# Two rows of w4 loaded amid the V stream in transfers of few partitions, and one closing copy in place of two

## The chip, the cores and the metric

The kernel runs on one core of a Trainium2 chip. The metric is the device time of one execution in microseconds (us); lower is better. All times below are us unless marked ns. Engines are called by the profile's names: PE is TensorE, DVE is VectorE, ACT is ScalarE, SP is SyncE, which here issues nearly all transfers. "Transfer engines" are the core's 16 DMA engines.

## The reference: one decode step of attention beside an MLP

The computation is one decode step for four sequences: layer norm, sliding-window attention with 32 query heads over 16 key/value heads (the last 2048 positions of the cache), and an MLP, summed. Cut to what matters here:

```python
# B=4, D=576, Hq=32, Hkv=16, Dh=128, window W=2048, F=4608, all bf16
xn = layernorm(x)                                # both branches read xn
q = xn @ wq
p = softmax(q k^T / sqrt(128))                   # k, v: [4, 16, last 2048 of 8192, 128]
attn = (p v) @ wo                                # wo: [4096, 576]
x1 = xn              # S=1: all four shifted groups of the mixer are zero, w1 and w2 drop out
h2 = gelu(layernorm(x1) @ w3) @ w4               # w3: [576, 4608], w4: [4608, 576]
out = x + attn + (x1 + h2)
```

The kernel reads about 87 MB and writes 4.6 KB: K and V windows make 67 MB of it, the weights the rest.

## The kernel before

**Stages.** The program loads wq and computes the queries; streams the 16 K tiles (2 MB each, one per key/value head, `kv_load`, line 98), with the MLP's first weight w3 among them, and accumulates all scores; takes one softmax over everything; streams the 16 V tiles the same way; and finishes with the rest of w4, the MLP's second weight. In the text, V4 or V13 is the V tile of that head, and wo2 to wo7 are the 0.6 MB pieces of the attention's output weight, one for two heads.

**Order of issue.** All large loads are issued by SP in program order; SP waits in front of each until its buffer is free. K and V share six buffers (`NKV`, line 17). Each transfer also signals a completion semaphore; in the program as built, SP's transfers use eight of these in turn, and an issue waits until the previous transfer on its semaphore has landed. This is the framework's doing and stands nowhere in the kernel's text. Counting back from V15 (line 438), the order is V10, wo5, V11, V12, wo6, V13, V14, wo7, V15.

**The V loop** (lines 435 to 443) issues tile v+4 while it computes head v: `v_compute` (64 matmuls), then `head_out`, whose later parts (selecting, projecting with wo into the accumulator `ACC`) are run one head later by `run_later`.

**w4.** It is held as two halves e of 18 rows per partition (`w4_src`, line 106). One "row" here is [128 partitions x 576] bf16, 1152 B per partition, 147 KB in all. `load_w4(e, i0, n, cuts)` (line 396) allocates one of the three buffers of pool `w` and issues one transfer per cut; `mlp_out` (line 407) multiplies each row into `ACC` by two matmuls (line 330). Nine rows are used before the softmax; at the end (line 444) come three loads: 9 rows, 9 rows, and 9 rows cut into 4, 2, 2, 1, named w4_0_9, w4_1_0 and w4_1_9 in the text by half and first row.

**The end.** After the last piece two copies move `ACC` (f32, 36 x 288) to `fin` (bf16): the left half by DVE, the right half by ACT (lines 456 and 457). Then SP and ACT each store one half of the output (line 459).

Of the kernel before, what the change touches and what calls it, by code (L numbers as in the profile page):

```python
# [11 lines left out]
BF16 = mybir.dt.bfloat16  # L12
# [9 lines left out]
def kernel(  # L22
# [18 lines left out]
    nc = tc.nc  # L41
    P = 128
    B, Sq, D = A_x.shape
# [19 lines left out]
    DH = D // 2  # L63
# [24 lines left out]
    wpl = ctx.enter_context(tc.tile_pool(name="w", bufs=NWP))  # L88
# [9 lines left out]
    def kv_load(win, h):  # L98
        t = kvp.tile([P, NCH, Dh], BF16, tag="kv")
        nc.sync.dma_start(out=t[:].rearrange("p c d -> p (c d)"),  # L100
                          in_=win[:, h].rearrange("b (p c) d -> p b (c d)", p=G))
        return t
# [3 lines left out]
    w4_src = B_w4.rearrange("(e m i) n -> e m i n", e=2, i=NFH)  # L106
# [72 lines left out]
    ACC = ps_acc.tile([P, 512], F32)  # L179
# [46 lines left out]
    for y in range(NY):  # L226
        tq = ps_o.tile([P, 2 * HB, P], BF16, tag="O", name=f"tq{y}")
        for k in range(2):
            for m in range(HB):
                nc.tensor.transpose(out=tq[:, k * HB + m, :],  # L230
                                    in_=q_rows[:, k, m, y, :, :].rearrange("p g i -> p (g i)"), identity=ident[:])
# [41 lines left out]
    def softmax():  # L273
        E = wpl.tile([P, NCH, NG, GK], F32, tag="w", name="E")
        mx = const.tile([P, NG], F32)
        nb = const.tile([P, 1], F32)
        sm = const.tile([P, NG], F32)
        for g in range(NG):
            nc.vector.reduce_max(out=mx[:, g:g + 1], in_=S[g][:], axis=AX.X)  # L279
        nc.vector.reduce_max(out=nb[:], in_=mx[:], axis=AX.X)  # L280
        nc.vector.tensor_scalar_mul(out=nb[:], in0=nb[:], scalar1=-scale)  # L281
        for g in range(NG):
            nc.scalar.activation(out=E[:, :, g, :].rearrange("p (c l) k -> p c k l", l=2),  # L283
                                 in_=S[g][:].rearrange("p (c k l) -> p c k l", k=GK, l=2), func=ACT.Exp, bias=nb[:], scale=scale, accum_out=sm[:, g:g + 1])
        rd = const.tile([P, 1], F32)
        nc.vector.tensor_reduce(out=rd[:], in_=sm[:], op=ALU.add, axis=AX.X)
        nc.vector.reciprocal(out=rd[:], in_=rd[:])
        rdm = const.tile([P, B], F32)
        nc.vector.tensor_scalar_mul(out=rdm[:], in0=mask[:], scalar1=rd[:])  # L289

        PZ = pzp.tile([P, NCH, P], BF16, tag="pz", name="PZ")
        HC = CP // 2
        for piece in range(NP):
            c0 = piece * CP
            pr = ktp.tile([P, CP, NG, GK, B], BF16, tag="kt", name=f"pr{piece}")
            for b in range(B):
                src = E[:, c0:c0 + CP, :, :].rearrange("p c g k -> p (c g k)")
                dst = pr[:, :, :, :, b].rearrange("p c g k -> p (c g k)")
                if b == 3 or (b == 1 and piece % 2):
                    nc.scalar.mul(out=dst, in_=src, mul=rdm[:, b:b + 1])  # L300
                else:
                    nc.vector.tensor_scalar_mul(out=dst, in0=src, scalar1=rdm[:, b:b + 1])  # L302
            for half in range(2):
                tp = ps_s.tile([P, HC, P], BF16, tag="S", name=f"pt{piece}{half}")
                for cc in range(HC):
                    nc.tensor.transpose(out=tp[:, cc, :],  # L306
                                        in_=pr[:, half * HC + cc, :, :, :].rearrange("p g k b -> p (g k b)"),
                                        identity=ident[:])
                dst = PZ[:, c0 + half * HC:c0 + (half + 1) * HC, :].rearrange("p c n -> p (c n)")
                src = tp[:].rearrange("p c n -> p (c n)")  # L310
                if half:
                    nc.scalar.copy(out=dst, in_=src)  # L312
                else:
                    nc.vector.tensor_copy(out=dst.bitcast(I32), in_=src.bitcast(I32))
        return PZ

    O_tiles = {}

    def v_compute(h):
        bank = ps_o.tile([P, 128], F32, tag="O", name=f"O{h}")  # L320
        O = bank[:, 0:B * rep].rearrange("p (b r) -> p b r", r=rep)
        O_tiles[h] = (O, bank[:, 64:64 + XR * rep * B].rearrange("p (x n) -> p x n", x=XR))
        vn = V_tiles.pop(h)
        for c in range(NCH):
            nc.tensor.matmul(out=O, lhsT=vn[:, c, :], rhs=PZ[:, c, :].rearrange("p (b n) -> p b n", b=B)[:, :, h * rep:(h + 1) * rep],  # L325
                             start=(c == 0), stop=(c == NCH - 1))
# [9 lines left out]
    def load_wo(g2):  # L336
        wo_tiles[g2] = wop.tile([P, XR, D], BF16, tag="wo", name=f"wo{g2}")
        nc.sync.dma_start(out=wo_tiles[g2][:].rearrange("p x n -> p (x n)"), in_=wo_src[:, g2, :])
# [3 lines left out]
    def head_out(h):  # L342


        O, T = O_tiles.pop(h)
        on = small.tile([P, rep, B], BF16, tag="on")
        nc.vector.tensor_copy(out=on[:].rearrange("p r b -> p b r"), in_=O)  # L347

        def select():
            for x in range(XR):  # L350
                nc.tensor.matmul(out=T[0:32, x, :], lhsT=ident[:, x:P:XR], rhs=on[:].rearrange("p r b -> p (r b)"),  # L351
                                 start=(x == 0), stop=(x == XR - 1), skip_group_check=True)
            g2, odd = divmod(h, 2)
            if not odd:
                onx_tiles[g2] = small.tile([P, XR, B], BF16, tag="onx", name=f"onx{g2}")
            onx = onx_tiles[g2]
            for r in range(rep):
                q = 32 * (2 * odd + r)
                nc.vector.tensor_copy(out=onx[q:q + 32, :, :], in_=T[0:32, :, r * B:(r + 1) * B])  # L359
            if odd:  # L360
                wt = wo_tiles.pop(g2)
                onx_tiles.pop(g2)

                def project():
                    for x in range(XR):
                        acc_matmuls(onx[:, x, :], lambda a, z, x=x: wt[:, x, a:z])
                later.append(project)
        later.append(select)

    def run_later():  # L370
        fns = later[:]
        later.clear()
        for fn in fns:
            fn()
# [21 lines left out]
    def load_w4(e, i0, n, cuts):  # L396
        t = wpl.tile([P, n, D], BF16, tag="w", name=f"w4_{e}_{i0}")
        parts = []
        a = 0
        for m in cuts:  # L400
            nc.sync.dma_start(out=t[:, a:a + m, :], in_=w4_src[e, :, i0 + a:i0 + a + m, :])
            parts.append((t[:, a:a + m, :], e, i0 + a, m))
            a += m
        assert a == n
        return parts

    def mlp_out(t, e, i0, n):
        for i in range(n):
            acc_matmuls(gT[:, e * NFH + i0 + i, :], lambda a, z, i=i: t[:, i, a:z])
# [22 lines left out]
        load_wo(g2)  # L432
    mlp_out(*w4[0])
    PZ = softmax()
    for v in range(Hkv):
        n = v + NV0
        if n < Hkv:
            V_tiles[n] = kv_load(v_win, n)
            if n % 2 == 0:
                load_wo(n // 2)  # L440
        run_later()
        v_compute(v)
        head_out(v)
    end = load_w4(0, 9, 9, (9,)) + load_w4(1, 0, 9, (9,)) + load_w4(1, 9, 9, (4, 2, 2, 1))
    run_later()
    mlp_out(*end[0])
    while later:
# [4 lines left out]

    fin = const.tile([P, DH], out.dtype)
    NR = 32 + B
    HH = DH // 2
    nc.vector.tensor_copy(out=fin[0:NR, 0:HH], in_=ACC[0:NR, 0:HH])  # L456
    nc.scalar.copy(out=fin[0:NR, HH:DH], in_=ACC[0:NR, HH:DH])  # L457
    for q, eng in ((0, nc.sync), (1, nc.scalar)):
        eng.dma_start(out=o2[:, q * DH:(q + 1) * DH], in_=fin[32 * q:32 * q + B, :])

# [29 lines left out]
```

## Time and profile before

| what | value |
|---|---|
| median of 3 runs | 217.47 us (217.23 to 218.13) |
| the profiled execution's own time | 217.53 us |
| its span, first to last instruction | 215.8 us |
| transferred | 87.52 MB, mean 406 GB/s |
| PE busy, DVE busy, ACT busy | 53%, 50%, 10% of the span |
| V tile, issue to landing (median of 16) | 29.1 us |
| mean granted PE clock | 0.668 |

The span is what the profile sees; the execution's time has 1.7 us around it. In the profile's rows, "SPq" is an issue by SP, "<-" after a bracketed number names what ended the engine's idle time, and a "granted clock" of 0.5 means that PE ran at half its speed in that stretch. A transfer is split into packets, here one per partition, and each transfer engine that took part marks its end by a completion record. A 128-partition transfer leaves 16 such records, and it has landed when the last one is there.

In the stretch tables the columns are: the stretch, its length, busy time of PE, of PE's weight loads, of DVE, ACT and POOL (with the number of instructions), the granted clock, the DMA share and GB/s.

### The profile page before, as it was taken

How to read it: one execution, taken by the hardware profiler on the slowest of the kernel's cores; microseconds unless marked ns; L12 is line 12 of the kernel's file. 1: busy time of each engine (PE TensorE's matmuls, PEld its weight loads, DVE VectorE, ACT ScalarE, POOL GpSimd, SP SyncE). 2: the span in 40 equal slices, each digit the busy share in tenths (PEclk: the TensorE clock that was granted, in tenths of full speed). 3: DMA queues.
4: the chain of work that ended last, by engine and by line, in shares of the span. 5: the costliest groups of instructions: out<-in, count | busy, mean ns of one | idle time of the engine just before them, and what ended most of it. 6: DMA issues, size and time to landing. Idle time of an engine off the chain costs nothing.

```text
span 215.8 us, 5535 instructions
## 1 busy us (share of the span) xinstructions
PE 114.9 (53%) x2577; PEld 74.2 (34%) x2577; DVE 108.7 (50%) x156; ACT 21.3 (10%) x37; POOL 1.8 (1%) x8
## 2 busy tenths in 40 slices
PE   0343788847544544455433097867662635445383
PEld 0110744526311111111101087747452534334341
DVE  7932968484999999989785591201000000000000
ACT  0202220000000000000003896000000000000000
POOL 1110000000000000000000000000000000000000
PEclk9999999658566665678578566555555555555559
DMA  6999999999999999999999999999999999999960
GB/s 250 431 427 424 418 429 444 409 436 416 427 422 434 416 425 431 416 434 437 403 438 422 434 406 428 430 419 428 413 431 427 405 436 415 436 418 426 415 253 14
DMA packets 8255, 87.52 MB, mean 406 GB/s; under 512 B 925, under 2 KB 1065, under 8 KB 2729
## 3 DMA queue, kind: packets, MB, share of 16 engines
q1 hardware_dynamic: 8216, 87.17, 96.0%
q8 instruction: 20, 0.33, 0.6%
q10 hardware_dynamic: 16, 0.01, 0.0%
q14 instruction: 3, 0.02, 0.0%
HBM read 87.17 MB, written 0.00 MB: 404 GB/s over the span
## 4 chain that ended last, share of the span: by engine, by line
DMA 70%; DVE 13%; PE 7%; ACT 5%; issue 3%; SPq 1%; DVEq 0%; ACTq 0%
DMA t<-in_A_k_cache_dram 36%; DMA t<-in_A_v_cache_dram 21%; DMA w<-in_B_w_dram 9%; DVE kt L258 6%; DMA wq<-in_A_wq_dram 3%; PE O L325 2%; ACT E L283 2%; PE pt L306 2%; ACT pr L300 2%; DVE qz L177 2%; PE qp L204 1%; ACT PZ L312 1%; DVE mx L279 1%; DVE pr L302 1%; PE ACC L330 1%
## 5 line engine op out<-in xcount | busy, mean ns | idle before, releaser
L258 DVE STREAM_TRANSPOSE kt<-t 128x2048 int32<-128x2048 int32 x32 | 72.3, 2293 | 12.6 <-DMA t<-in_A_k_cache_dram 12.4
L267 PE MATMUL S<-kt,qz 32*32 32x512 bf16 x1024 | 36.9, 625 | 37.7 <-DVE kt L258 36.2
L325 PE MATMUL O<-PZ,t 128*128 128x8 bf16 x1024 | 30.5, 168 | 26.2 <-DMA t<-in_A_v_cache_dram 22.8
L325 PEld LDWEIGHTS <-t 128*128 128x128 bf16 x1024 | 29.1, 104 | 30.2 <-DMA t<-in_A_v_cache_dram 25.4
L347 DVE CAST on<-O 128x8 bf16<-128x8 f32 x16 | 2.7, 167 | 58.0 <-PE O L325 57.9
L267 PEld LDWEIGHTS <-qz 32*32 32x32 bf16 x1024 | 10.7, 95 | 60.3 <-issue 57.1
L306 PE MATMUL pt<-ident,pr 128*128 128x128 bf16 x64 | 6.7, 291 | 9.4 <-DVE pr L302 8.3
L383 PEld LDWEIGHTS <-w 128*128 128x128 bf16 x144 | 9.3, 165 | 5.2 <-DMA w<-in_B_w_dram 2.7
L383 PE MATMUL ACC<-ln2T,w 128*128 128x4 bf16 x144 | 9.6, 202 | 1.8 <-DMA w<-in_B_w_dram 1.8
L330 PE MATMUL ACC<-wo,onx 128*4 128x288 bf16 x64 | 9.0, 437 | 2.2 <-DVE onx L359 2.2
L283 ACT ACTIVATE E<-S,nb 128x512 f32<-128x512 f32 x4 | 4.0, 1116 | 59.3 <-DVE nb L281 59.3
L306 PEld LDWEIGHTS <-pr 128*128 128x128 bf16 x64 | 5.9, 135 | 10.0 <-ACT pr L300 10.0
L300 ACT ACTIVATE pr<-E,rdm 128x512 bf16<-128x512 f32 x6 | 8.1, 1430 | 0.8 <-DVE rdm L289 0.8
L359 DVE CAST onx<-O 32x16 bf16<-32x16 f32 x32 | 5.3, 165 | 5.3 <-PE O L351 4.9
L457 ACT CAST fin<-ACC 36x144 bf16<-36x144 f32 x1 | 0.3, 273 | 77.4 <-DVE fin L456 77.4
L330 PE MATMUL ACC<-w,gT 128*4 128x288 bf16 x72 | 7.3, 362 | 0.9 <-DMA w<-in_B_w_dram 0.9
L302 DVE TENSOR_SCALAR pr<-E,rdm 128x512 bf16<-128x512 f32 x10 | 6.4, 787 | 0.3 <-PE pt L306 0.2
L204 PE MATMUL qp<-wq,xnT 128*4 128x512 bf16 x32 | 4.0, 620 | 4.5 <-DMA wq<-in_A_wq_dram 4.5
L224 DVE CAST q_rows<-qp 128x256 bf16<-128x256 f32 x8 | 2.9, 410 | 6.4 <-PE qp L204 6.4
L351 PE MATMUL O<-on,ident 128*32 128x8 bf16 x64 | 4.2, 171 | 3.6 <-DVE on L347 3.6
L351 PEld LDWEIGHTS <-ident 128*32 128x32 bf16 x64 | 4.4, 111 | 3.4 <-issue 3.1
L330 PEld LDWEIGHTS <-gT 128*4 128x4 bf16 x72 | 3.9, 103 | 4.7 <-issue 2.2
(68 smaller groups left out, 54.5 us busy)
## 6 DMA issues: line engine op xcount, KB each, us to landing
t<-in_A_k_cache_dram SPq DMA_DIRECT2D x16, 2048.0 KB, 24.7
t<-in_A_v_cache_dram SPq DMA_DIRECT2D x16, 2048.0 KB, 29.1
w<-in_B_w_dram SPq DMA_DIRECT2D x4, 1152.0 KB, 13.1
wo<-in_A_wo_dram SPq DMA_DIRECT2D x8, 576.0 KB, 21.5
wq<-in_A_wq_dram SPq DMA_DIRECT2D x4, 1024.0 KB, 6.3
w<-in_B_w_dram SPq DMA_DIRECT2D x3, 1296.0 KB, 30.4
w_t<-in_B_w_dram SPq DMA_DIRECT2D x1, 576.0 KB, 14.3
w<-in_B_w_dram SPq DMA_DIRECT2D x1, 576.0 KB, 25.2
```

The source lines that it names most:

```text
L204: nc.tensor.matmul(out=qp[k][32 * i:32 * i + B, :], lhsT=lhsT, rhs=rhs, start=False, stop=False, skip_group_check=True)
L258: nc.vector.transpose(out=ap32(kt, e * G * 2, [[2 * G * 2, NCH // 2], [1, 2], [2, G]]), in_=ap32(kn, e * G, [[2 * 2 * G, NCH // 2], [2 * G ...
L267: nc.tensor.matmul(out=S[g][32 * b:32 * b + 32, :].rearrange("p (c k l) -> p c k l", k=GK, l=2), lhsT=qz[32 * g:32 * g + 32, b, h, y, :], ...
L283: nc.scalar.activation(out=E[:, :, g, :].rearrange("p (c l) k -> p c k l", l=2), in_=S[g][:].rearrange("p (c k l) -> p c k l", k=GK, l=2), ...
L300: nc.scalar.mul(out=dst, in_=src, mul=rdm[:, b:b + 1])
L302: nc.vector.tensor_scalar_mul(out=dst, in0=src, scalar1=rdm[:, b:b + 1])
L306: nc.tensor.transpose(out=tp[:, cc, :], in_=pr[:, half * HC + cc, :, :, :].rearrange("p g k b -> p (g k b)"), identity=ident[:])
L325: nc.tensor.matmul(out=O, lhsT=vn[:, c, :], rhs=PZ[:, c, :].rearrange("p (b n) -> p b n", b=B)[:, :, h * rep:(h + 1) * rep], start=(c == 0 ...
L330: nc.tensor.matmul(out=ACC[32 * q:32 * q + B, 0:DH], lhsT=lhsT, rhs=rhs_cols(q * DH, (q + 1) * DH), start=False, stop=False, skip_group_ch ...
L351: nc.tensor.matmul(out=T[0:32, x, :], lhsT=ident[:, x:P:XR], rhs=on[:].rearrange("p r b -> p (r b)"), start=(x == 0), stop=(x == XR - 1), ...
L359: nc.vector.tensor_copy(out=onx[q:q + 32, :, :], in_=T[0:32, :, r * B:(r + 1) * B])
L383: nc.tensor.matmul(out=gp[:, fc, :], lhsT=lhsT, rhs=rhs, start=False, stop=False, skip_group_check=True)
```

## The change

Rows 16 and 17 of w4's second half are no longer loaded at the end. A buffer `w4_end` is allocated before the V loop, and ahead of V10 and of V13 one row each is loaded into it, split by partitions into transfers of 8, 4, 12, 2, 6 and 96 partitions, and of 10, 14, 1, 3, 5, 7 and 88. At the end the remaining seven rows of the half are loaded in cuts of 4, 2 and 1; the two early rows are multiplied after w4_1_0 and before the 4-row piece. The two closing copies become one on DVE over all 288 columns. No value of the result is computed differently.

```diff
@@ the V loop
+    end_t = wpl.tile([P, 9, D], BF16, tag="w", name="w4_end")
+    groups = {10: (8, (8, 4, 12, 2, 6, 96)), 13: (7, (10, 14, 1, 3, 5, 7, 88))}
     for v in range(Hkv):
         n = v + NV0
+        if n in groups:
+            i, parts = groups[n]
+            p0 = 0
+            for k in parts:
+                nc.sync.dma_start(out=end_t[p0:p0 + k, i, :], in_=w4_src[1, p0:p0 + k, 9 + i, :])
+                p0 += k
+            assert p0 == P
         if n < Hkv:
             V_tiles[n] = kv_load(v_win, n)
...
-    end = load_w4(0, 9, 9, (9,)) + load_w4(1, 0, 9, (9,)) + load_w4(1, 9, 9, (4, 2, 2, 1))
+    end = load_w4(0, 9, 9, (9,)) + load_w4(1, 0, 9, (9,)) + [(end_t[:, 7:9, :], 1, 16, 2)]
+    for a, m in ((0, 4), (4, 2), (6, 1)):
+        nc.sync.dma_start(out=end_t[:, a:a + m, :], in_=w4_src[1, :, 9 + a:9 + a + m, :])
+        end.append((end_t[:, a:a + m, :], 1, 9 + a, m))
...
-    HH = DH // 2
-    nc.vector.tensor_copy(out=fin[0:NR, 0:HH], in_=ACC[0:NR, 0:HH])
-    nc.scalar.copy(out=fin[0:NR, HH:DH], in_=ACC[0:NR, HH:DH])
+    nc.vector.tensor_copy(out=fin[0:NR, :], in_=ACC[0:NR, 0:DH])
```

## The prediction

> **What bounds the kernel now.** First the page's chain and its row of transfer-engine shares.
>
> ```profile
> DMA  6999999999999999999999999999999999999960
> q1 hardware_dynamic: 8216, 87.17, 96.0%
> q8 instruction: 20, 0.33, 0.6%
> DMA 70%; DVE 13%; PE 7%; ACT 5%; issue 3%; SPq 1%; DVEq 0%; ACTq 0%
> ```
>
> The transfer engines are full from the second slice almost to the end, so time is bytes plus whatever leaves an engine without work. All 16 do not end together; the stretches of the tail show it:
>
> ```profile
> 204.00:206.00 2.00, 1.02 (x23) 0.81 (x22) 0.50 (x3) 0.00 (x0) 0.00 (x0) 0.50 1.02 416
> 206.00:208.00 2.00, 2.00 (x22) 1.07 (x18) 0.00 (x0) 0.00 (x0) 0.00 (x0) 0.50 0.68 272
> 208.00:210.00 2.00, 2.00 (x20) 1.10 (x18) 0.00 (x0) 0.00 (x0) 0.00 (x0) 0.50 0.49 184
> 210.00:212.00 2.00, 1.78 (x28) 1.01 (x24) 0.00 (x0) 0.00 (x0) 0.00 (x0) 0.99 0.15 51
> ```
>
> The last two columns are the DMA share and GB/s: from 208 on half of the engines have nothing left. The completion records of the last transfer agree: eight engines between 207.00 and 207.98, five at 210.1 to 210.4 or 211.6, three more by 211.93. The lateness comes in steps of about 1.57: a 16 KB instruction packet (q8) takes 1.02 to 1.11 on its engine, and the data packet after it 1.08 to 1.16 where 16 KB otherwise takes 0.61. The q8 durations repeat with period eight, so eight engines share the 20 fetches, two or three each. The latest engine sets the end.
>
> Third, SyncE's issues beside TensorE's work.
>
> ```profile
> 172.26 1.87 PE L325 MATMUL O<-PZ,t 128*128 128x8 bf16 x64 [0.97 <-DMA t<-in_A_v_cache_dram]
> ...
> 172.23 0.54 SPq L100 DMA_DIRECT2D t<-in_A_v_cache_dram  x1
> ...
> 186.18 0.33 SPq L401 DMA_DIRECT2D w<-in_B_w_dram  x1
> ```
>
> The first is head 10's compute, released by V10's landing at 172.21. The second is the issue of V15, with no matmul that it needs: it waits for the same landing. The program as built gives SP's transfers eight completion semaphores in turn, so each issue waits until the transfer eight places earlier has landed. V15 is eight after V10; the third row, a two-row piece of w4, is eight after wo6 and dates wo6's landing: 186.16. Eight in flight are now mostly 2 MB each, so nothing runs dry.
>
> **The change, part by part.** Thirteen small transfers take places in that ring of eight, although they hold 0.29 MB together.
>
> *First group (6, before V10).* V10's issue now follows wo4's landing (162.39) instead of 148.0. 0.54 to issue and some 0.6 to its first packet give 163.5; the earliest engine ends V9 at 163.84 by its completion, so nothing is lost there. One row spread evenly is 8 packets of 1152 B at 0.051 = 0.41 per engine, ahead of all that follows: wo6 lands near 186.6.
>
> *Second group (7, after wo6, before V13).* Places back from V13: seven small ones, then wo6. V13 may be issued only when wo6 has landed, and behind wo6 there is nothing in the queues but small rows. Before, V13 was issued at 161.00, 25 us ahead. Behind it on SP stand V14, wo7, V15 and all of w4's end, and TensorE, done with head 12 by 188, waits for V13. Now every engine runs out: the early ones from about 182, the latest at 186.6. The price from landing to effective restart is bounded by two rows. The program's first load (wq_t, 0.5 MB, idle engines) lands 3.4 after its issue by the page; its packets are 8 of 0.159 = 1.27 per engine: 2.1 of fixed time, and 2.2 with V's issue of 0.54 for 0.42. The closing store took 1.44 from issue (212.93) to landing with 0.04 of packets: 1.4, or 1.6 with V's issue. [...] I take 1.9, between the rows and nearer the load, which is the same sort of transfer. Bounds 0.9 to 2.2.
>
> *What is late next.* All 16 engines restart level. Work from V13 to the end is, per engine, 24 packets of 16 KB at 0.6135 (14.7), wo7 1.43, two times 8 x 0.389 (6.2), and 8 packets each of 0.1785, 0.0935 and 0.0515 (2.6): 25.0. Before, the engine that was latest at wo6 had had its third fetch, and no more. In the records three fetches come after 188 (188.97, 199.87, 209.18), on engines that were 1.4 us earlier. Level engines lose that lead, so one fetch, 1.57, comes on top. End of transfers: 186.6 + 1.9 + 25.0 + 1.57 = 215.1, against 211.93 now: +3.15. Without the fetch on top (it falls in the dry stretch) 213.5; with the restart at its bounds 214.1 to 215.4.
>
> [...]
>
> *Last pieces.* w4's end transfers are 4, 2, 1 rows instead of 4, 2, 2, 1. The two early rows are multiplied after w4_1_0 and before the 4-row piece.
>
> ```profile
> 208.73 2.64 PE L330 MATMUL ACC<-w,gT 128*4 128x288 bf16 x30
> 211.59 0.67 PE L330 MATMUL ACC<-w,gT 128*4 128x288 bf16 x6 [0.22 <-DMA w<-in_B_w_dram]
> 212.30 0.30 DVE L456 CAST fin<-ACC 36x144 bf16<-36x144 f32 x1 [7.00 <-PE ACC L330]
> 212.63 0.27 ACT L457 CAST fin<-ACC 36x144 bf16<-36x144 f32 x1 [77.41 <-DVE fin L456]
> ```
>
> TensorE is nearly the bound there: 36 matmuls after w4_1_0 with 0.22 idle. A row (two matmuls) takes 0.24 by the records' starts at granted clock 0.5 and 0.12 at 1.0, which came at 210.1. After the change the last piece lands 2.6 after w4_1_0 instead of 3.24 (two rows less to transfer), with the same 18 rows to multiply. These need 4.3 at 0.5 throughout and 2.2 at 1.0, so TensorE may end 0.33 (as now) to 1.7 after the last landing. With the clock rising midway, 0.75: +0.4. Bounds 0 to +1.4.
>
> *Closing copy.* Two 36x144 copies run one behind the other, 212.30 to 212.91 = 0.61. VectorE's casts of 8, 144 and 256 f32 columns take 0.167, 0.301 and 0.410, 0.98 ns a column; 288 come to 0.44. Gain 0.17, on the path.
>
> SP's extra issues (some 13 x 0.38 = 5 us) cost nothing by themselves: SP waits for landings meanwhile. The buffer of w4_end is free since the MLP's first stage.
>
> *Sum.* 3.15 + 0.4 - 0.17 = +3.4 on the profiled execution's 217.53 (span 215.8 and 1.7 around it): 220.9. The shown median, 217.47, is the same within 0.1.
>
> **Rivals.**
> 1. *The restart is paid, but no fetch falls on top.* For it: one fetch came at 188.97, close to the dry stretch. Against: two more follow on other engines. +3.4 - 1.57: 219.3.
> 2. *The wait is hidden*: wo6 lands early enough, or the rows cover it, and lateness among engines absorbs it. For it: eight engines have 3 to 5 us to spare. Against: the latest has none. Only the tail moves, +0.4 - 0.17 at most: 217.5.
> [...]
> 4. *The tail on a cold TensorE*: clock 0.5 to the end, +1.0 beyond mine: 221.9. In the profile the clock stayed at 0.5 for 78 us before 210.1.
>
> **How the numbers follow.** Forecast 220.9, 0.68; rival 1 0.10; rival 4 0.10; rival 2 0.08; rival 3 0.04. The range starts at rival 1 less 0.4 for the tail's bound, 218.9, and ends at rival 4 with the restart's upper bound, 222.2; it leaves out rivals 2 and 3. 0.5% of the time, 1.1 us, is what a measurement can tell from no change. Slower 0.88, same 0.10 (rival 2 and most of rival 3), faster 0.02.
>
> **What would show it.** V13's issue right after wo6's landing near 186.6, its landing near 193.5 to 195 instead of 191.2; a slice near 182 to 188 with the DMA share far below full; completions of wo7 almost level; the last landing near 215; fewer than 0.5 us from TensorE's end to the output's issue. Wrong if V13 is issued well before 180, or if the DMA share shows no gap.

## The result, and the profile after

| | before | after |
|---|---|---|
| median, same chip (4 runs each) | 217.62 us (217.23 to 218.13) | 221.39 us (221.21 to 221.50) |
| profiled execution, its span | 217.53, 215.8 | 221.50, 219.7 |
| last landing | 211.93 | 215.85 |
| PE's end, output's issue | 212.26, 212.93 | 216.62, 217.14 |
| mean granted PE clock | 0.668 | 0.664 |

The change makes the kernel slower by 3.77 us, a ratio of 1.0168 with a 95% interval of 1.0151 to 1.0184. The profiled execution lost 3.97.

The page after, as before: the share of the transfer engines and their GB/s in 40 slices of 5.5 us, and the chain that ended last.

```profile
DMA  6999999999999999999999999999999995799990
GB/s 260 447 404 437 418 429 433 411 421 433 422 424 430 424 430 424 427 424 420 437 425 427 430 411 429 424 418 426 424 383 374 428 424 211 299 430 424 416 373 6
...
DMA 66%; DVE 13%; PE 11%; ACT 4%; SPq 2%; issue 2%; DVEq 0%; ACTq 0%
```

Two slices that were full before stand at 5 and 7 tenths, and 211 and 299 GB/s: 181 to 192 us. A smaller dent is in the GB/s alone, 383 and 374 in the slices of 159 to 170, where the DMA share stays at 9: engines are busy there and move less. The chain's shares hardly tell of it: DMA 66% instead of 70, PE 11 instead of 7, and waiting at issues (SPq and issue) 4 as before. The place is found in the slices.

The stretches around the dent in the changed kernel (columns as before: the clock, the DMA share and GB/s are the last three):

```profile
180.00:184.00 4.00, 2.65 (x74) 2.37 (x76) 0.50 (x3) 0.00 (x0) 0.00 (x0) 0.50 0.86 355
184.00:188.00 4.00, 2.73 (x74) 2.10 (x70) 0.17 (x1) 0.00 (x0) 0.00 (x0) 0.50 0.27 91
188.00:190.00 2.00, 0.00 (x0) 0.00 (x0) 0.33 (x2) 0.00 (x0) 0.00 (x0) 0.50 0.78 270
190.00:196.00 6.00, 1.46 (x54) 1.46 (x55) 0.00 (x0) 0.00 (x0) 0.00 (x0) 0.50 1.02 431
...
212.00:214.00 2.00, 2.00 (x20) 1.02 (x18) 0.00 (x0) 0.00 (x0) 0.00 (x0) 0.50 0.92 345
214.00:216.00 2.00, 2.00 (x26) 1.28 (x24) 0.00 (x0) 0.00 (x0) 0.00 (x0) 0.68 0.05 19
```

The engines run out from 182 on, and from 184 to 188 they work a quarter of the time. The last two rows are the other half of the story: before, the tail from 206 on went 272, 184, 51 GB/s, as engines finished one after the other; now it is nearly full to 214, and almost nothing is left after.

Who made the dent stands in SyncE's timeline (start, duration, engine, line, operation, tiles, count; a long duration is an issue that waits):

```profile
170.28 0.58 SPq L338 DMA_DIRECT2D wo<-in_A_wo_dram  x1
170.92 14.93 SPq L444 DMA_DIRECT2D w_end<-in_B_w_dram  x7
186.96 1.61 SPq L100 DMA_DIRECT2D t<-in_A_v_cache_dram  x2
188.68 0.57 SPq L338 DMA_DIRECT2D wo<-in_A_wo_dram  x1
189.30 0.54 SPq L100 DMA_DIRECT2D t<-in_A_v_cache_dram  x1
```

wo6 is issued, then the seven small pieces, and V13 only at 186.96, 0.01 after the last completion of wo6 (186.95). V14, wo7 and V15 follow at once, since they had only stood behind it. Before, V13 and V14 had been issued 26 us earlier:

```profile
161.00 2.47 SPq L100 DMA_DIRECT2D t<-in_A_v_cache_dram  x2
```

And what the wait does to TensorE:

```profile
185.59 1.87 PE L325 MATMUL O<-PZ,t 128*128 128x8 bf16 x64 [0.99 <-DMA t<-in_A_v_cache_dram]
...
194.54 1.87 PE L325 MATMUL O<-PZ,t 128*128 128x8 bf16 x64 [6.57 <-DMA t<-in_A_v_cache_dram]
```

The first row is head 12, the second head 13: 6.57 idle, released by V13's landing (194.50). The completions of V13 lie within 0.48 of each other, where wo6's were 3.66 apart: the dry stretch has levelled the engines.

The tail:

```profile
213.31 2.21 PE L330 MATMUL ACC<-w,gT 128*4 128x288 bf16 x18
215.35 1.27 PE L330 MATMUL ACC<-w_end,gT 128*4 128x288 bf16 x18
216.66 0.45 DVE L468 CAST fin<-ACC 36x288 bf16<-36x288 f32 x1 [6.83 <-PE ACC L330]
217.14 0.30 SPq L470 DMA_DIRECT2D out_dram<-fin  x1
```

The second row holds the eighteen matmuls of the last nine rows, four of them for the two early rows, which landed long ago. TensorE comes to them only at 215.35, behind w4_1_0, and ends 0.78 after the last landing (215.85). One copy of 0.45 stands where two stood, and the output is issued 0.52 after TensorE's end instead of 0.67.

### The profile page after: what moved, and what is told of

Same layout as the page of the kernel before. It is cut to its first block, busy times and chain, and to the rows that moved or that the text cites. A ratio compares the mean times of both kernels' runs of the same rounds, so it can differ in the third digit from the quotient of the medians.

```text
span 219.7 us, 5546 instructions
## 1 busy us (share of the span) xinstructions
PE 114.5 (52%) x2577; PEld 73.3 (33%) x2577; DVE 108.9 (50%) x156; ACT 21.1 (10%) x36; POOL 1.8 (1%) x8
## 4 chain that ended last, share of the span: by engine, by line
DMA 66%; DVE 13%; PE 11%; ACT 4%; SPq 2%; issue 2%; DVEq 0%; ACTq 0%
DMA t<-in_A_k_cache_dram 35%; DMA t<-in_A_v_cache_dram 18%; DMA w<-in_B_w_dram 9%; DVE kt L258 6%; PE O L325 3%; PE ACC L330 3%; DMA wq<-in_A_wq_dram 3%; PE pt L306 2%; ACT E L283 2%; DVE qz L177 2%; PE qp L204 1%; ACT PZ L312 1%; ACT pr L300 1%; DVE mx L279 1%; DVE pr L302 1%
## 5 line engine op out<-in xcount | busy, mean ns | idle before, releaser
L306 PE MATMUL pt<-ident,pr 128*128 128x128 bf16 x64 | 5.5, 259 | 9.0 <-DVE pr L302 7.6
L306 PEld LDWEIGHTS <-pr 128*128 128x128 bf16 x64 | 4.9, 118 | 9.9 <-ACT pr L300 9.9
L330 PE MATMUL ACC<-w,gT 128*4 128x288 bf16 x54 | 6.8, 436 | 0.7 <-DMA w<-in_B_w_dram 0.7
L330 PEld LDWEIGHTS <-onx 128*4 128x4 bf16 x64 | 3.8, 110 | 4.3 <-DVE onx L359 2.6
```

The source lines that it names most:

```text
L306: nc.tensor.transpose(out=tp[:, cc, :], in_=pr[:, half * HC + cc, :, :, :].rearrange("p g k b -> p (g k b)"), identity=ident[:])
L330: nc.tensor.matmul(out=ACC[32 * q:32 * q + B, 0:DH], lhsT=lhsT, rhs=rhs_cols(q * DH, (q + 1) * DH), start=False, stop=False, skip_group_ch ...
```

## The experiments

Two theories stood at first. The **ring theory**: the thirteen small transfers cost by the places that they take among SP's eight completion semaphores, and only the second group does, by making V13 wait for wo6. Its rival: **the small transfers cost by themselves**, by their spread over few engines or by the partitions that they reach. A third question was the tail. "Small" is said of a piece of a row of w4; each difference is against the kernel before on the same chip (its medians there were 217.48 and 217.70).

**1. The two rows, each in one transfer.** Same bytes, places and tail, no split.

```diff
-    groups = {10: (8, (8, 4, 12, 2, 6, 96)), 13: (7, (10, 14, 1, 3, 5, 7, 88))}
+    groups = {10: (8, (128,)), 13: (7, (128,))}
```

> The two early rows come as one 128-partition transfer each, at the same places; everything else as in the changed kernel. Ring theory (thirteen small transfers fill the eight places in flight, so V13 waits for wo6 and all engines run dry): V13's issue goes back to about 161 to 164, no slice of the DMA share falls below 9 before 206, the last landing is near 211.9 and the time 217.3 to 217.8 (before, less 0.17 for the copy, plus 0 to 0.4 for the longer end of TensorE). Rival, that bringing the rows early or the new order of the last pieces costs the time: 221, as in the changed kernel.

217.67 against 217.48, a ratio of 1.0005 (0.9985 to 1.0025): no loss that can be measured. So moving two rows forward, the new cuts at the end and the copy cost nothing together, and the whole 3.8 comes with the split. SP's timeline of this run:

```profile
162.84 0.33 SPq L444 DMA_DIRECT2D w_end<-in_B_w_dram  x1
167.73 1.21 SPq L100 DMA_DIRECT2D t<-in_A_v_cache_dram  x2
```

V13 is issued at 167.73, 19 us earlier than in the changed kernel. That is later than the 161 to 164 expected: the two whole rows take places too, so eight back from V13 stands V9, which lands at 167.72. This shows that the split is the cause, and leaves open which of its two effects.

**2. The same thirteen pieces, issued by POOL.** Issued there, the pieces take no place in SP's ring: V13 is issued at 162.82, where it was 161.00 before and 186.96 in the changed kernel.

```diff
-                nc.sync.dma_start(out=end_t[p0:p0 + k, i, :], in_=w4_src[1, p0:p0 + k, 9 + i, :])
+                nc.gpsimd.dma_start(out=end_t[p0:p0 + k, i, :], in_=w4_src[1, p0:p0 + k, 9 + i, :])
```

> The same thirteen few-partition transfers, issued by GpSimd, which has completion semaphores of its own, so that they take no place among SP's eight; they will be issued as soon as their buffer is free, in the K stage. Ring theory: 217.3 to 217.8. Rival, that few-partition transfers cost by themselves (packets of 1152 B, uneven engines, a fixed time for each): the rows are as uneven and as small as before, so about 221, or at least 218.5.

218.95 against 217.48, 1.0058 (1.0038 to 1.0078): +1.47, above what the ring theory gave and within what its rival gave ("at least 218.5"). Off SP's ring 2.3 of the 3.77 are gone, and 1.47 stay. POOL issued the pieces between 52 and 68, while K was streaming, and there the GB/s dip. Its stretches:

```profile
64.00:68.00 4.00, 2.01 (x64) 0.66 (x64) 3.06 (x2) 0.00 (x0) 1.06 (x2) 0.50 1.03 380
...
72.00:76.00 4.00, 1.13 (x32) 0.33 (x32) 3.18 (x3) 0.00 (x0) 0.00 (x0) 0.52 1.02 371
```

In experiment 1 these two stretches moved 414 and 422 at DMA shares of 0.99 and 1.01. Of K's 467 packets of 16 KB that start between 60 and 80 us, 171 took longer than 0.64, against 2 of 518 in experiment 1. POOL's way of issuing may have a price of its own; whole rows through POOL were not tried, so this run alone doesn't settle the size.

**3 and 4. Six and five pieces in the second group.** With six, V13's place eight back is V12; with five, it is V11, which lands 5 us before.

Six:

```diff
-    groups = {10: (8, (8, 4, 12, 2, 6, 96)), 13: (7, (10, 14, 1, 3, 5, 7, 88))}
+    groups = {10: (8, (8, 4, 12, 2, 6, 96)), 13: (7, (10, 14, 1, 3, 12, 88))}
```

> Second group in six transfers instead of seven (10, 14, 1, 3, 12, 88), so eight places before V13 stands V12 and not wo6. Ring theory: V13 is issued at V12's landing, about 185.5; wo6 (1.4 us of work) and the small rows are still queued, so the dry time of the latest engine shrinks by about 1.4 while all engines still restart nearly level: 219.5 to 220.3. Rival, few-partition transfers cost by themselves: one less of thirteen, 221.1.

Five:

```diff
-    groups = {10: (8, (8, 4, 12, 2, 6, 96)), 13: (7, (10, 14, 1, 3, 5, 7, 88))}
+    groups = {10: (8, (8, 4, 12, 2, 6, 96)), 13: (7, (10, 14, 4, 12, 88))}
```

> Second group in five transfers (10, 14, 4, 12, 88), so eight places before V13 stands V11. Ring theory: V13 is issued at V11's landing, about 180.6, with V12 and wo6 (6.3 us of work) still queued; the latest engine does not run dry, the early ones idle a little, which costs nothing: 217.3 to 218.2. Rival, few-partition transfers cost by themselves: two less of thirteen, 220.8.

Six: 220.91, 1.0144 (1.0112 to 1.0175), +3.43. The expectation was 0.6 to 1.4 too low. V13 was issued at 186.15, only 0.8 earlier than with seven, because V12 lands just ahead of wo6 on the latest engines. Only wo6's 0.6 MB are behind V12, so the engines ran dry all the same: a DMA share of 0.43 and 144 GB/s from 184 to 188.

Five: 218.71, 1.0055 (1.0035 to 1.0074), +1.23. SP's row of V13 and V14 in this run:

```profile
180.94 6.28 SPq L100 DMA_DIRECT2D t<-in_A_v_cache_dram  x2
```

V13 is issued at 180.94, right behind V11's landing (180.92), 3 us before the earliest engine completes its last small piece (184.21). On the engine that was latest, V13 ends 5.0 after wo6 (193.14 against 188.14), which is the 4.92 that its eight packets take: nothing ran dry. The step from six pieces to five is thus worth 2.2 us (220.91 less 218.71): one place in the ring, and the pieces of 1 and 3 partitions joined into one of 4. But 1.2 remain with no dry stretch, where the ring theory allowed 0.7 at most. That is the second effect again, here in SP's own queue.

**5 and 6. Half and half: by partitions and by columns.** Four transfers of 73 KB in both; only the direction of the cut differs.

By partitions:

```diff
-    groups = {10: (8, (8, 4, 12, 2, 6, 96)), 13: (7, (10, 14, 1, 3, 5, 7, 88))}
+    groups = {10: (8, (64, 64)), 13: (7, (64, 64))}
```

> [...] Two theories on the 1.0 us that remained in the five-transfer kernel, where 16 KB packets took 0.65 to 0.8 and more instead of 0.61 while small transfers ran. If the slowing comes from engines writing into partitions that another engine is writing (crossed partitions): the GB/s in the stretches 161:168 and 181:189 fall below 424 at a full DMA share, by up to 40, and the time is 218.0 to 218.7. If it comes from the number of transfers or from uneven engines: 420 to 430 GB/s and 217.3 to 217.9, as with whole rows.

By columns:

```diff
-    groups = {10: (8, (8, 4, 12, 2, 6, 96)), 13: (7, (10, 14, 1, 3, 5, 7, 88))}
+    groups = {10: (8, (288, 288)), 13: (7, (288, 288))}
...
-                nc.sync.dma_start(out=end_t[p0:p0 + k, i, :], in_=w4_src[1, p0:p0 + k, 9 + i, :])
+                nc.sync.dma_start(out=end_t[:, i, c0:c0 + k], in_=w4_src[1, :, 9 + i, c0:c0 + k])
```

> [...] If crossed partitions are the cause: 420 to 430 GB/s in 181:189 and 217.4 to 218.0. If two transfers in place of one, or smaller packets, are the cause: 219 again.

By partitions: 219.26 against 217.48, 1.0090 (1.0063 to 1.0118). By columns: 217.69 against 217.70, 0.9999 (0.9984 to 1.0015). Halves by partitions cost more than the 0.5 to 1.2 expected; halves by columns cost nothing. Both use all 16 engines: the two transfers more than in experiment 1 left 32 more completion packets in q1 (8392 against 8360). So the spread over few engines is not needed for the loss. What differs is the direction of the cut: a half by partitions reaches 64 of them, a half by columns all 128. Halves by partitions, in the stretch with the first row and that with the second:

```profile
161.00:168.00 7.00, 2.13 (x68) 2.07 (x68) 0.49 (x3) 0.00 (x0) 0.00 (x0) 0.50 1.02 389
181.00:189.00 8.00, 5.25 (x144) 4.34 (x143) 0.91 (x6) 0.00 (x0) 0.00 (x0) 0.50 1.02 378
```

And by columns:

```profile
161.00:168.00 7.00, 2.70 (x92) 2.63 (x93) 0.49 (x3) 0.00 (x0) 0.00 (x0) 0.50 1.03 424
181.00:189.00 8.00, 4.50 (x117) 3.58 (x114) 0.99 (x6) 0.00 (x0) 0.00 (x0) 0.50 1.03 427
```

The share is full in all four rows; where the cut is by partitions, the GB/s lack 8 and 11%. The packets say the same: of V's 16 KB packets after 135 us, 187 of 1432 took longer than 0.64 there, against 8 of 1431 before and 36 of 1433 in experiment 1; 170 of the 187 start between 161 and 169 or between 181 and 189, where the pieces pass. So it isn't the small transfers' own time that costs, but that V's packets become slow while they pass. The text calls this **crossing**; the expectations speak of crossed partitions, after a guess at the cause. Why the packets become slow is not shown by any run, and no record tells which partitions an engine writes.

**7. Crossing alone.** The thirteen pieces, one ahead of each V tile from V4 on and the last after V15, so that V13 never waits for what is near.

```diff
-    groups = {10: (8, (8, 4, 12, 2, 6, 96)), 13: (7, (10, 14, 1, 3, 5, 7, 88))}
+    groups = {4: (8, 0, 8), 5: (8, 8, 4), 6: (8, 12, 12), 7: (8, 24, 2), 8: (8, 26, 6), 9: (8, 32, 96), 10: (7, 0, 10), 11: (7, 10, 14), 12: (7, 24, 1), 13: (7, 25, 3), 14: (7, 28, 5), 15: (7, 33, 7), 16: (7, 40, 88)}
```

> All thirteen few-partition transfers on SP's queue, but one ahead of each V tile from V4 on and the last behind V15, so that never more than three of the eight places in flight are small. Ring theory: no dry stretch, V13's landing less than 5.2 after wo6's on the latest engine. What is left is the crossed partitions alone: 218.2 to 219.0, as with five transfers in the second group. If the crossing counted only where many small ones follow each other: 217.4 to 217.9.

219.16 against 217.70, 1.0064 (1.0041 to 1.0086): +1.46, 0.2 above the upper end of what crossing was expected to cost. Two of its stretches:

```profile
161.00:168.00 7.00, 2.13 (x68) 2.06 (x68) 0.49 (x3) 0.00 (x0) 0.00 (x0) 0.50 1.01 393
181.00:189.00 8.00, 5.38 (x144) 4.47 (x144) 0.99 (x6) 0.00 (x0) 0.00 (x0) 0.50 1.01 423
```

There is no dry stretch, and in the first one the same full share with few GB/s.

**8. The ring alone.** Row 17 whole ahead of V10; row 16 ahead of V13 in seven transfers cut by columns, so that each reaches all partitions.

```diff
-    groups = {10: (8, (8, 4, 12, 2, 6, 96)), 13: (7, (10, 14, 1, 3, 5, 7, 88))}
+    groups = {10: (8, (576,)), 13: (7, (96, 80, 80, 80, 80, 80, 80))}
...
-                nc.sync.dma_start(out=end_t[p0:p0 + k, i, :], in_=w4_src[1, p0:p0 + k, 9 + i, :])
+                nc.sync.dma_start(out=end_t[:, i, c0:c0 + k], in_=w4_src[1, :, 9 + i, c0:c0 + k])
```

> [...] Ring theory: V13 again waits for wo6, all engines run dry, restart level and one fetch comes on top, so most of the loss stays: 219.7 to 220.8, the rest of the 3.8 us being the crossed partitions. If the dry stretch was the smaller part: below 219.

221.14 against 217.70, 1.0156 (1.0132 to 1.0179): +3.44, 0.3 above the upper end of what the ring alone was expected to give. Its stretches:

```profile
180.00:184.00 4.00, 2.40 (x72) 2.23 (x74) 0.50 (x3) 0.00 (x0) 0.00 (x0) 0.50 0.87 344
184.00:188.00 4.00, 2.75 (x74) 2.11 (x71) 0.17 (x1) 0.00 (x0) 0.00 (x0) 0.50 0.30 78
```

and SP's rows:

```profile
163.20 22.93 SPq L444 DMA_DIRECT2D w_end<-in_B_w_dram  x7
187.24 1.84 SPq L100 DMA_DIRECT2D t<-in_A_v_cache_dram  x2
```

This is the changed kernel's dent, with V13 issued at 187.24 and landed between 194.31 and 194.75. As far as the runs can tell, the ring alone costs as much as the change: +3.44 (2.9 to 3.9 by its interval) against +3.77 (3.3 to 4.0). Crossing does not come on top: 3.44 and 1.46 would make 4.9.

The landings show why. wo4 has landed before the first small piece moves, and wo6 is what V13 waits for. From the last completion of wo4 to that of wo6 it took 23.77 before, 24.27 in the changed kernel, and 24.40 and 24.04 in experiments 1 and 8, whose transfers all reach 128 partitions. In experiments 3, 4 and 5, whose pieces reach fewer, it took 25.37, 25.73 and 25.29 (in experiment 7, whose pieces pass from V4 to the end, 24.27). So in the changed kernel crossing hardly touched the latest landing, which starts V13. A likely reason, not shown by itself: the largest piece of the second group, 88 partitions, is held there until 185.56 by V12's landing and passes when little of wo6 is left; in experiments 3 and 4 it is issued at 180.78 and 174.53. Crossing made the early landings late (from the first completion of wo4 to that of wo6 24.54, against 22.85 in experiment 1), and engines that are early only wait longer in the dry stretch.

**9. The early rows multiplied early.** `mlp_out` of the two rows ahead of head 15, while TensorE waits for V15.

```diff
+        if v == Hkv - 1:
+            mlp_out(end_t[:, 7:9, :], 1, 16, 2)
...
-    end = load_w4(0, 9, 9, (9,)) + load_w4(1, 0, 9, (9,)) + [(end_t[:, 7:9, :], 1, 16, 2)]
+    end = load_w4(0, 9, 9, (9,)) + load_w4(1, 0, 9, (9,))
```

> The changed kernel, but the two early rows are multiplied in front of head 15's compute, where TensorE waits for V15 anyway, and not after w4_1_0. Tail theory (TensorE had 18 rows left after w4_1_0 and ended 0.77 after the last landing instead of 0.33): it ends 0.33 to 0.4 after it again, 221.0 (220.7 to 221.2). Rival, that TensorE's order is hidden behind the transfers: 221.4, as in the changed kernel.

221.12 against 217.48, 1.0165 (1.0142 to 1.0188). Its tail:

```profile
214.61 1.27 PE L330 MATMUL ACC<-w_end,gT 128*4 128x288 bf16 x14
215.93 0.45 DVE L470 CAST fin<-ACC 36x288 bf16<-36x288 f32 x1 [6.32 <-PE ACC L330]
```

With four matmuls fewer in the tail TensorE ends 0.33 after the last landing (215.56) instead of 0.78. But the granted clock rose from 0.5 to 1.0 at 213.4 here, just behind w4_1_0's landing (213.10), and only at 215.3 in the changed kernel. Experiment 8 kept the changed kernel's order and all eighteen matmuls; its clock rose at 213.6, and there too TensorE ended 0.33 after the last landing (216.11):

```profile
214.72 1.72 PE L330 MATMUL ACC<-w_end,gT 128*4 128x288 bf16 x18
```

So this run doesn't show what the four matmuls are worth: the moment at which the clock rose is enough for the 0.45. The medians (+3.64 here, +3.77 in the changed kernel) lie too close to tell.

**10. The closing copy alone**, in the kernel before.

```diff
-    HH = DH // 2
-    nc.vector.tensor_copy(out=fin[0:NR, 0:HH], in_=ACC[0:NR, 0:HH])
-    nc.scalar.copy(out=fin[0:NR, HH:DH], in_=ACC[0:NR, HH:DH])
+    nc.vector.tensor_copy(out=fin[0:NR, :], in_=ACC[0:NR, 0:DH])
```

> The kernel before with the one closing copy and nothing else. The two copies ran one behind the other (0.61), one of 288 columns took 0.45 in the changed kernel's trace: 217.3, 0.16 below before, which the timing hardly tells from nothing; the profile should show the output's issue 0.5 after TensorE's end instead of 0.67. Rival, that ScalarE's copy was hidden: no difference in the profile.

217.75 against 217.70, 1.0002 (0.9989 to 1.0016). The rows:

```profile
212.12 0.45 DVE L455 CAST fin<-ACC 36x288 bf16<-36x288 f32 x1 [7.15 <-PE ACC L330]
212.60 0.34 SPq L457 DMA_DIRECT2D out_dram<-fin  x1
```

TensorE ends at 212.08 and the output is issued 0.52 later (0.67 before): 0.15 is there in the profile, and too little for the timing to show.

**11 and 12. An attempt to use the spread.** Some engines are early at the end, and the five completions of the 5-partition piece are all early (last section). The thirteen pieces left a completion record for each partition up to 14, 16 for 96 partitions and 11 for 88, which fits equal shares: six partitions on each of 16 engines, eight on each of 11. By these counts a transfer of 125 partitions would go to five engines, 25 on each; this is an estimate, and that the five would be the early ones was assumed. Three rows of w4 were brought that way, ahead of V10, with the last three partitions ahead of V12; the control brings them in one transfer of 128 partitions. Both multiply them before head 15 and cut the end into 3, 2 and 1.

125 and 3 partitions:

```diff
-    groups = {10: (8, (8, 4, 12, 2, 6, 96)), 13: (7, (10, 14, 1, 3, 5, 7, 88))}
+    groups = {10: (0, 125), 12: (125, 128)}
...
+            nc.sync.dma_start(out=end_t[p0:p1, 6:9, :], in_=w4_src[1, p0:p1, 15:18, :])
```

> An attempt to beat both kernels. [...] If lateness belongs to the engine and crossed partitions cost little: 216.1 (215.8 to 216.6). If crossed partitions slow the other engines: the 0.43 MB cost 1.5 times as much as the 0.29 MB of the small transfers, 217.0 to 218.5.

Control:

```diff
-    groups = {10: (0, 125), 12: (125, 128)}
+    groups = {10: (0, 128)}
```

> The same three rows early in one 128-partition transfer ahead of V10, multiplied in front of head 15, and one closing copy: all engines carry the same as before. By both theories only the copy is gained: 217.3 (217.1 to 217.6). It is what the five-engine kernel is to be compared with.

125 and 3 partitions: 219.76 against 217.48, 1.0104 (1.0080 to 1.0127), worse than either outcome expected. Control: 217.60, 1.0004 (0.9987 to 1.0020). The stretches with the transfer of 125:

```profile
161.00:165.00 4.00, 2.01 (x68) 1.94 (x67) 0.49 (x3) 0.00 (x0) 0.00 (x0) 0.50 1.01 356
165.00:169.00 4.00, 0.00 (x0) 0.00 (x0) 0.00 (x0) 0.00 (x0) 0.00 (x0) 0.50 1.07 256
```

A DMA share of 1.07 beside 256 GB/s: everything is busy, and slow. The 125 packets of 3456 B in that transfer took 0.232 on the mean, where the same rows took 0.137 in the control. That this is crossing again is the reading that fits experiments 5 to 7; the run by itself shows only the slowness. No version tried was measurably faster than the kernel before.

## Why the prediction was right, step by step

The likeliest case came true: 221.39 against 220.9. The terms, each against what was measured:

- **The wait.** "V13 may be issued only when wo6 has landed": 0.01 apart in the trace. Experiments 4 and 8 confirm it from both sides: with five places instead of seven there is no dry stretch, and seven transfers cut by columns bring all of it back.
- **wo6's landing.** Forecast 186.6, measured 186.95. Of these 0.35, 0.29 were there before any small piece moved: wo4 landed at 162.68 in this execution and at 162.39 before. From there to wo6 it took 0.50 longer than before, where the forecast's bytes make 0.41. What the forecast didn't have is crossing: 384 GB/s between 161 and 168, where it was 430 before. It weighed the small transfers by bytes and engines alone, and not by what they do to V's packets (64 of the 148 of 16 KB that start in that stretch took longer than 0.64, against 2 of 176 before). That this spared the latest landing (experiment 8) is luck.
- **The restart.** Forecast 1.9, bounds 0.9 to 2.2. For the lower bound 0.7 of the store's 1.6 was counted as covered by the group's rows, a share that no run shows: in the trace the group's last data packet starts at 187.23 and V13's first at 188.57. From wo6's landing to the middle of V13's completions (194.26) there are 7.3, less 4.92 for V13's packets: 2.4, over the upper bound. V13's first packets start at 188.6, 1.64 after its issue starts, and on four engines 0.3 later; twelve of the sixteen take 0.78 to 1.26 where 0.61 is usual. The same sum gives 2.4 in experiment 8, but 2.0 in experiment 9, whose transfers are those of the changed kernel and where the first packets took 0.62 to 0.86. So the term was 0.5 too small in this trace and 0.1 in that one; what makes the difference is open. Slow first packets were within the upper bound: the program's first load, which gave it, had them too (0.40 to 0.69 on the first twelve, where 0.16 is usual).
- **The work behind V13.** 20.1 per engine after V13's own eight packets; measured from its earliest completion to the earliest of the last transfer 20.03 (194.02 to 214.05).
- **The fetch on top.** Forecast 1.57, on one engine. Fifteen engines complete the last transfer between 214.05 and 214.49, one at 215.85, 1.6 behind the middle of the others. Its fetch came at 203.25. An earlier one, at 186.80, fell into the dry stretch and cost nothing, which is what rival 1 was about; there were enough of them for one to fall behind it. So it was in experiments 8 and 9, at 203.47 and 203.00.
- **The last landing.** 215.1 forecast, 215.85 measured. The 0.75 are wo6's 0.35 and the restart's 0.5, less 0.1 in the work.
- **The tail.** Forecast 0.75 after the last landing, measured 0.78; the clock rose at 215.3, midway, which is the condition that the forecast had set. That it did so in this execution is luck: with the same 36 matmuls behind w4_1_0 the tail was 0.33 in experiment 8, where the clock rose as w4_1_0 landed, and 1.14 in experiment 6, where it rose 2.6 later.
- **The copy.** Forecast 0.44 long and 0.17 saved; 0.45 and 0.15. One sign was missed by a little: from TensorE's end to the output's issue it took 0.52, not under 0.5.

By these, the output's issue came 4.21 later (217.14 against 212.93), where the forecast had 3.4. The execution grew by 3.97, since what follows the issue took 0.3 less of the span (2.56 against 2.87), and the medians differ by 3.77. So the two terms that were too small account for the 0.8 that the trace shows over the forecast; the median, 221.39 against 220.9, shows 0.5.

Of the rivals, "the wait is hidden" (217.5) and rival 3, a faster kernel (0.04), fell with the dent. That rows spread unevenly relieve the late engines is not shown by any run; what the runs show is that the transfer of 125 partitions cost 2.16 against its control (219.76 and 217.60, experiments 11 and 12). The cold tail (221.9) lies nearest to the result in time, yet the clock did rise, and what made up the difference were the restart and wo6.

The completion records tell how many engines a piece had: in the changed kernel 8, 4, 12, 2, 6 and 16 for the pieces of the first group, and 10, 14, 1, 3, 5, 7 and 11 for those of the second, 99 in all. Which engines these were no record tells.

Four things stay open: why V's packets are slow during crossing; why crossing spares the latest landing in the changed kernel and not in experiments 3 to 5; why the restart took 2.0 in one run and 2.4 in two others; and how much of experiment 2 is POOL's own way of issuing.

## What to carry to other kernels

In a program built like this one a transfer costs a place in a ring as well as its bytes: before small transfers are put amid large ones, count eight issues back from each large one and ask what must have landed, and what is still in flight behind that. Where a piece must be cut, cut it along the free dimension and keep all 128 partitions: halves by partitions cost 1.8 us here, and halves by columns nothing that could be measured. In these runs a stretch with a full DMA share and low GB/s (1.02 and 378 in experiment 5) was a sign of crossing, and one with a low share (0.27 in the changed kernel) a wait at the issue. What crossing costs depends on where it falls: about 1.2 to 1.8 us in the kernels without a dry stretch, and nothing that can be told in the changed kernel.

## What the runs showed that was not expected

- **The direction of a cut.** Halving two rows by partitions, 0.29 MB of 87.5, cost 1.8 us; halving them by columns cost nothing (217.69 against 217.70).
- **Which engines are late.** In the changed kernel the pieces themselves tell: at 184 to 187 the 5-partition piece has five completions within 0.62; the 7-partition piece has five early ones within 0.63 and two that come 1.4 behind them; the 14-partition piece has seven early and seven late. That the five engines of the first piece are the five early ones of the second is an assumption, since no record names its engine.
- **A restart from dry can be dearer than the first load.** It took 2.4 us with 16 KB packets in the changed kernel and in experiment 8, and 2.0 in experiment 9, where the first load gave 2.2 at most. The slow first packets are up to 0.65 of it in the changed kernel (1.26 against 0.61).
- **How much the tail depends on the clock.** With the same work behind w4_1_0, TensorE ended 0.33 to 1.14 us after the last landing, later the later the clock rose (experiments 8 and 6, and the changed kernel between them with 0.78).
